# Bulk loads on one queue, q's place, products per unit and the gate's place in a convolution and attention kernel

## Chip, cores and metric

The kernel runs on one NeuronCore of a Trainium2 chip. The metric is the device time of one execution in microseconds (us). TensorE (PE) multiplies matrices into PSUM; VectorE (DVE) and ScalarE (ACT) copy and compute; GpSimd (POOL) prepares masks and, like SyncE (SP) and ACT, can issue DMAs. The 16 DMA engines move the data of all queues: POOL's issues go to queue q0, SP's to q1, ACT's to q10.

## The reference

All inputs are bf16, with S = 2048 positions and D = 640 channels. Here x is `A_q`, F a long convolution and att an attention over 8 keys.

```python
g = sigmoid((x * gate_w).sum(-1))
kv = (4-tap causal convolution of A_k with A_shift_k) * A_v
y = F(kv, A_ssm_k) + kv * A_ssm_D     # causal, as long as S, by FFT of length 2 S
a = x * y
b = att(x @ B_wqkv) @ B_wo            # 32 heads of 20; keys at i, i-2, ..., i-14
out = g * a + (1 - g) * b
```

## The kernel before

The program is written out by a planner. Each part of the work is a generator that yields requests (`Req`: engine, cost in ns, the events that it depends on, and for a DMA `move`, the time of its transfer). `Plan.run` (L195) takes the request with the smallest key, its earliest start plus 120 ns times a priority from `PRI` (L143), and only then the instruction is written into the program. So the planner's costs and due times set the order on every engine and every queue; on the chip each engine runs its list in order and waits for what the data need. The model of DMA has a `pipe` per queue (L158: SP, POOL and ACT apart) that transfers fill one after the other, and a `lane` of at most 8 transfers in flight.

The work in order of time:

- `loads` (L352) brings x and the weights in on SP. `heads` (L414) writes constants and masks on POOL. `xpose` transposes x on PE, and `vproj` (L512) and `qkproj` (L559) multiply it by the weights. The results of `qkproj` go through two staging tiles (`stg`).
- `fragger` (L598) moves rows of `stg` by 72 DMAs on SP, most of 20 rows and about 85 KB, to `qb` and `kb`: each head gets a place on 32 partitions. Four heads make a set, and there are 8 sets in three buffers.
- `score_gen` (L620) multiplies a set block by block, ACT takes exponentials (L627, 80 of them), and `pv_gen` (L648, L657, L660) multiplies by v and divides.
- `bulk` (L363) issues on POOL the loads of k, v and ssm_k (tile `h_lin`), 24 DMAs of 320 KB with contiguous pieces of 320, 160 and 128 bytes. `conv` (L465, L472) and `conv_v` (L476) compute kv on DVE.
- `gate` computes sigmoid. Its row goes by four small DMAs on SP (L535) from a part of tile `KX` to `g_nat`.
- `load_G` (POOL) puts the constant matrix G of the second stage into tile `SX`, columns 10240 to 18432. The transform of ssm_k of the first half (P = 0) lies in columns 0 to 10240. `load_T` (POOL) loads `wo` and the constant T.
- `h_stream` and `u_stream` (P = 0 and 1) transform ssm_k and kv: first stage `s1_unit` (L681), second stage `s2_unit` (L697), 11 units of 3 or 2 columns of 160 outputs, each copied out of PSUM by ACT or DVE (L274, L276). `swaps` (L768, L770) writes by DMA a copy `Hw` of the ssm_k side with its halves exchanged.
- `mults` (L781) multiplies on DVE the transforms: 16 products of 2560 elements a partition, each half P only after all of its transforms and its swaps.
- `inverse1` (L793) and `final` (L871) are the two stages back. `op_tr` (L811) and `outproj` (L827, L831) do the attention's output product, with 1 - g applied in ACT's copy.
- `load_q` (L843) loads x once more as `qg`, in 4 DMAs of 640 KB on POOL, into columns 0 to 10240 of `SX`. These hold data that `inverse1(0)` reads, so it waits for the last of that. `qscale` (L850) multiplies `qg` by g in 16 DVE instructions. For each of six groups of row tiles `final` copies out of PSUM on ACT (L878, two copies of up to 960 elements), multiplies by `qg` (L883), adds the attention's part (L885) and issues four DMAs on SP to the output (L888).

Of the kernel before, what the change touches and what calls it, by code (L numbers as in the profile page):

```python
# [47 lines left out]
WARM = 8  # L48

# [80 lines left out]
class Req:  # L130


    def __init__(self, engs, cost=0.0, deps=(), take=0, give=(), n=0, move=0.0, pri=None, mode=None, mm=0, lean=0.0):
        self.engs, self.cost, self.deps, self.take, self.give, self.n, self.move = engs, cost, deps, take, give, n, move
        self.pri, self.mode, self.mm, self.lean = pri, mode, mm, lean
# [14 lines left out]
class Plan:  # L150


    def __init__(self, nslots):
        self.at = dict(P=0.0, A=0.0, D=0.0, G=0.0, S=0.0, Q=0.0)
        self.mode = None
        self.count = 0
        self.page = 0.0
        self.pipe = {"S": 800.0, "G": 0.0, "Q": 0.0}  # L158
        self.lane = {"S": [], "G": [], "Q": []}
        self.slots = [Bank() for _ in range(nslots)]  # L160
        self.streams = []
        self.log = []
# [9 lines left out]
    def start(self, r, e):  # L172
# [10 lines left out]
        if r.move and len(self.lane[e]) >= 8:  # L183
            t = max(t, self.lane[e][-8])
        return t
# [9 lines left out]
    def run(self):  # L195
        while self.streams:
# [50 lines left out]
def kernel(  # L247
# [96 lines left out]
    def load(name, dst, src, us, deps=(), q="S"):  # L344
        g = yield Req(q, 700.0 if q != "G" else 300.0 + 0.7 * us, deps, move=us)
# [6 lines left out]
    def loads():  # L352
        yield from load_x(0)
        yield from load("Wv0", Wv[:, 0:3], W3[:, 0:3, 2, :], 1800.0)
        yield from load_x(1)
        yield from load("W0", Wqk[:, :, 0, :], W3[:, :, 0, :], 3000.0)
        yield from load_x(2)
        yield from load_x(3)
        yield from load("W1", Wqk[:, :, 1, :], W3[:, :, 1, :], 3000.0)
        for a in range(4, 8):  # L360
            yield from load_x(a)

    def bulk():  # L363
        for c in (1, 0):
            for q in range(4):
                yield from load(f"k{q}{c}", kin[32 * q:32 * q + 32, 3 + 32 * c:35 + 32 * c, :],
                                raw(k2, 32 * c * D + QC * q, [[64 * D, 32], [D, 32], [1, QC]]), 2200.0, [ev("x3")], "G")
# [9 lines left out]
        for c in range(2):  # L377
            for q in range(4):
                yield from load(f"v{q}{c}", vin[32 * q:32 * q + 32, c], raw(v2, QC * q + 80 * c, [[64 * D, 32], [D, 64], [1, 80]]), 2300.0, (), "G")
        yield Req("G", 1.0, [ev("xtr")])  # L380
        h_lin = p0.tile([128, 80, 2, 64], BF, name="h_lin", tag="HL")
        st["h_lin"] = h_lin
        for c in range(2):
            for q in range(4):
                yield from load(f"h{q}{c}", h_lin[32 * q:32 * q + 32, :, c, :],
                                raw(A_ssm_k, (160 * q + 80 * c) * S, [[64, 32], [S, 80], [1, 64]]), 2300.0, (), "G")

    def load_G():
        yield Req("G", 1.0, [ev("conv"), ev("grow"), ev("vproj")])
# [24 lines left out]
    def heads():  # L414
# [27 lines left out]
        plan.at["G"] = 19000.0  # L442
# [135 lines left out]
    def fragger():  # L578
# [4 lines left out]
        for ft in range(NDT):  # L583
            for w in range(2):
# [5 lines left out]
                for h in range(f0 // DH, (f0 + 127) // DH + 1):  # L590
# [6 lines left out]
                    g = yield Req("S", 720.0, deps, move=rows * 300.0 / eng)  # L597
# [109 lines left out]
    def transform(key, P):  # L707
# [109 lines left out]
    def outproj():  # L817
# [4 lines left out]
        for t in range(16):  # L822
# [14 lines left out]
    def load_q():  # L837
        yield Req("G", 1.0, [ev("i10")])
        qg = st["SX"][:, 0:16 * D].rearrange("p (t n) -> p t n", t=16)
        st["qg"] = qg  # L840
        for g in range(4):
            r = yield Req("G", 1200.0, move=2000.0)
            nc.gpsimd.dma_start(qg[32 * g:32 * g + 32], raw(x2, (32 * (g // 2) + g % 2) * D, [[64 * D, 32], [2 * D, 16], [1, D]]))  # L843
        mark("qg", r)

    def qscale():
        for t in range(16):
# [81 lines left out]
```

## Time and profile before

| | |
|---|---|
| median of 3 runs | 282.65 us (281.76 to 283.15) |
| the profiled execution | 282.82 us, its span 281.0 us |
| mean granted clock of PE | 0.84 |
| busy, share of the span | PE 77%, DVE 68%, ACT 58%, POOL 22% |
| DMA, share of 16 engines | q0 (POOL) 29.0%, 14.84 MB; q1 (SP) 26.3%, 18.04 MB |
| chain that ended last | PE 43%, DVE 26%, DMA 23%, SP's queue 3% |

The span is the profiled execution from its first to its last instruction. The chain is followed back from the last instruction to what released it at each step. A stretch of the span is shown with the busy time of each engine, the granted clock of PE (1.0 is full speed) and the share of time in which the DMA engines worked. A row of the timeline gives start, duration, engine, line, operation, output and input, and in brackets the idle time before it and what ended it.

### The profile page before, as it was taken

To read this page: it belongs to the slowest core of one execution; us is meant where nothing else is said; L and a number is where in the kernel's file an instruction comes from. 1 tells how busy PE (TensorE), PEld (TensorE's weight loads), DVE (VectorE), ACT (ScalarE), POOL (GpSimd) and SP (SyncE) were. 2 spreads that over 40 slices of the span, in tenths; PEclk is the share of its full clock that TensorE was granted. 3 is DMA by queue.
4 is the path that set the end of the run, shared out by engine and by line. 5 is a ranking of instruction groups with operands and counts; after the bars stand their busy time and mean duration, and the time that the engine had idled before them with its cause. 6 is when DMAs were issued, how large, how long until landed. Compare 5 with 4: busy or idle time off the path is not lost.

```text
span 281.0 us, 8233 instructions
## 1 busy us (share of the span) xinstructions
PE 216.7 (77%) x3654; PEld 166.9 (59%) x3654; DVE 189.8 (68%) x213; ACT 161.8 (58%) x197; POOL 60.5 (22%) x79
## 2 busy tenths in 40 slices
PE   6999999216900898999985999888999999991320
PEld 2999975103700466775663778777887789971210
DVE  2142079940502899999885878999998995411992
ACT  1333543033801387886884878999965588771460
POOL 5799999323301000000400000000000000300000
PEclk9999999755975599999955557999999999996555
DMA  6953999999995114233598100019579000495085
GB/s 221 333 208 81 168 169 166 157 166 200 153 101 84 25 42 89 52 72 76 159 266 243 51 3 2 3 39 220 122 155 220 5 0 2 87 197 94 11 213 156
DMA packets 13034, 33.81 MB, mean 120 GB/s; under 512 B 2764, under 2 KB 6872, under 8 KB 12360
## 3 DMA queue, kind: packets, MB, share of 16 engines
q0 software_dynamic: 4368, 14.84, 29.0%
q1 hardware_dynamic: 8072, 18.04, 26.3%
q8 instruction: 28, 0.46, 0.7%
q10 hardware_dynamic: 560, 0.42, 0.5%
q14 instruction: 6, 0.05, 0.1%
HBM read 20.01 MB, written 2.62 MB: 81 GB/s over the span
## 4 chain that ended last, share of the span: by engine, by line
PE 43%; DVE 26%; DMA 23%; SPq 3%; issue 2%; POOL 1%; ACT 1%; DVEq 0%
PE psv L512 9%; DMA kb<-stg 8%; PE op L827 7%; PE pj L559 6%; DMA g_nat<-KX 5%; DMA SX<-in_A_q_dram 5%; PE s L697 5%; DMA qb<-stg 5%; DVE UC L276 4%; PE sc L620 4%; PE i L793 4%; DVE Hs L276 3%; DVE stg L276 3%; DVE KX L465 3%; PE O L648 3%; DVE SX L885 2%
## 5 line engine op out<-in xcount | busy, mean ns | idle before, releaser
L627 ACT ACTIVATE ETall<-sc 121x912 bf16<-121x912 f32 (+1 forms) x80 | 64.3, 855 | 22.1 <-PE sc L620 21.2
L559 PE MATMUL pj<-xT,Wqk 128*128 128x342 bf16 (+1 forms) x300 | 51.6, 326 | 15.5 <-DVE oS L660 15.1
L559 PEld LDWEIGHTS <-Wqk 128*128 128x128 bf16 x300 | 28.8, 101 | 32.6 <-issue 16.4
L620 PE MATMUL sc<-qb,kb 31*128 31x114 bf16 x576 | 25.4, 242 | 18.0 <-DMA kb<-stg 16.8
L465 DVE TENSOR_TENSOR KX<-KX 128x1760 bf16<-128x1760 bf16 (+1 forms) x24 | 24.8, 1042 | 11.6 <-DMA KX<-in_A_k_dram 11.2
L620 PEld LDWEIGHTS <-kb 31*128 31x128 bf16 x576 | 14.6, 104 | 29.4 <-issue 20.0
L274 ACT CAST stg<-pj 128x684 bf16<-128x684 f32 (+1 forms) x13 | 9.5, 744 | 36.9 <-DMA kb<-stg 27.6
L472 DVE TENSOR_TENSOR KX<-KX 128x1760 bf16<-128x1760 bf16 (+1 forms) x18 | 18.8, 1044 | 15.9 <-DMA g_nat<-KX 15.4
L512 PE MATMUL psv<-KX,xT 128*121 128x320 bf16 x180 | 25.7, 299 | 1.4 <-DVE xT L276 1.4
L274 ACT CAST UC<-s 128x1024 bf16<-128x1024 f32 (+1 forms) x24 | 22.6, 1000 | 4.0 <-PE s L697 3.0
L512 PEld LDWEIGHTS <-xT 128*121 128x121 bf16 x180 | 23.6, 134 | 2.0 <-issue 1.2
L274 ACT CAST VW<-psv 121x640 bf16<-121x640 f32 x18 | 12.5, 695 | 21.0 <-PE psv L512 21.0
L827 PE MATMUL op<-wo,oT 128*128 128x512 bf16 (+1 forms) x160 | 23.5, 304 | 0.0
L697 PEld LDWEIGHTS <-SX 64*128 64x128 bf16 x512 | 20.2, 99 | 5.1 <-issue 3.3
L843 POOL DMA_DIRECT2D SX<-in_A_q_dram x4 | 2.6, 668 | 94.1 <-ACT UC L274 94.1
L276 DVE CAST stg<-pj 128x726 bf16<-128x726 f32 (+1 forms) x17 | 15.2, 894 | 11.1 <-DMA g_nat<-KX 10.3
L276 DVE CAST UC<-s 128x960 bf16<-128x960 f32 (+2 forms) x18 | 19.9, 1139 | 1.1 <-PE s L697 1.0
L276 DVE CAST SX<-s 128x1024 bf16<-128x1024 f32 (+1 forms) x16 | 18.8, 1195 | 2.5 <-PE s L697 1.9
L827 PEld LDWEIGHTS <-oT 128*128 128x128 bf16 x160 | 16.5, 147 | 5.7
L793 PE MATMUL i<-F,Hw 128*128 128x128 bf16 x160 | 18.3, 219 | 0.0
L831 ACT ACTIVATE bl<-op,omg 128x640 bf16<-128x640 f32 x16 | 12.7, 795 | 9.2 <-PE op L827 9.2
L793 PEld LDWEIGHTS <-Hw 128*128 128x128 bf16 x160 | 17.9, 113 | 0.0
(74 smaller groups left out, 370.4 us busy)
## 6 DMA issues: line engine op xcount, KB each, us to landing
xn<-in_A_q_dram SPq DMA_DIRECT2D x8, 320.0 KB
KX<-in_A_k_dram POOLq DMA_DIRECT2D x8, 320.0 KB, 9.7
vin<-in_A_v_dram POOLq DMA_DIRECT2D x8, 320.0 KB, 13.6
h_lin<-in_A_ssm_k_dram POOLq DMA_DIRECT2D x8, 320.0 KB, 17.2
Hw<-SX SPq DMA_DIRECT2D x4, 640.0 KB
Hw<-Hs SPq DMA_DIRECT2D x4, 640.0 KB
SX<-in_A_q_dram POOLq DMA_DIRECT2D x4, 640.0 KB, 10.2
out_dram<-SX SPq DMA_DIRECT2D x20, 120.0 KB
```

The costliest lines, as they stand in the source:

```text
L274: nc.scalar.copy(dst, src)
L276: nc.vector.tensor_copy(dst, src)
L465: eng.tensor_tensor(d, kin[:, n + 3 - j:n + 3 - j + m, :], w.to_broadcast([128, m, QC]), ALU.mult)
L472: eng.tensor_tensor(ta if j else dst, ta, tb, ALU.add)
L512: nc.tensor.matmul(ps[0:BK, n0 // 320, 0:320], lhsT=xT[:, dt, s0:s0 + BK], rhs=Wv[:, dt, n0:n1], start=(dt == 0), stop=(dt == NDT - 1))
L559: nc.tensor.matmul(ps[:, i, 0:n], lhsT=Wqk[:, dt, w, 128 * ft:128 * ft + 128], rhs=xT[:, dt, s0:s0 + n], start=(dt == 0), stop=(dt == NDT ...
L620: nc.tensor.matmul(sc[:, hh, BQ * bb:BQ * bb + BQ], lhsT=kb[r:r + DH + NF, BK * b:BK * b + 128], rhs=qb[r:r + DH + NF, BQ * b:BQ * b + BQ] ...
L627: nc.scalar.activation(ETall[0:BK, e, :, 0:BQ * nb], sc[0:BK, :, 0:BQ * nb], ACT.Exp, scale=SCALE)
L697: nc.tensor.matmul(ps[:, c, 160 * jj:160 * jj + 160], lhsT=st["G"][rows, j0 + jj, rr, :], rhs=Am[rows, rr].rearrange("p o (q j) l -> p j ( ...
L793: nc.tensor.matmul(d, lhsT=st[(key, P)][:, c, o + il // 4, :, il % 4], rhs=M[:, k, :], start=(k == 0), stop=(k == 1), skip_group_check=True)
L827: nc.tensor.matmul(op[:, n0:n1], lhsT=oT[:, ft].rearrange("p h m a -> p a (h m)")[:, t, :], rhs=wo[:, ft, n0:n1], start=(ft == 0), stop=(f ...
L831: nc.scalar.activation(bl[:, t, :], op[:, 0:D], ACT.Copy, scale=omg[:, t:t + 1])
```

## The change

k, v, ssm_k, G, wo, T and q are issued on SP instead of POOL. The planner now has a single `pipe` for all queues. A bulk load (one with `bg`) is placed no sooner than when the modelled backlog of the pipe is below BG = 1236 ns, and behind a request of priority 0 that could start at the same time. This is an order in SP's list; the program holds no wait for it. SP and ACT share one list of 8 transfers in flight. The new requests for G, wo, T, ssm_k and q on SP ("Req("S", 1.0, [...])") keep an issue behind its conditions in the plan.

q's tile `qg` moves to columns 8192 to 18432 of `SX`. Row tiles 4 to 15 lie in G's columns and are loaded when all four transforms' second stages are done, tiles 0 to 3 when `inverse1(0)` is done, each in four DMAs on SP. `final` and `outproj` take tiles 4 to 15 first.

`mults` becomes `products`: each unit of the second stage of kv is multiplied as soon as its copy and the swaps of its half P are done, 44 products of 960 or 640 elements in runs of 12 or 8.

`qscale` goes. `final` applies g as the per-partition scale of ACT's copies, which are now one for each row tile and half, 32 of 320 elements. All priorities and preferences of the planner (`PRI`, `LEAN_*`) have new values, and some modelled costs do.

```diff
+BG = 1236.0
...
-LEAN_QK = -370.0
-LEAN_V = 53.0
-LEAN_H = 195.0
-PRI = dict(loads=0, fragger=0, xpose=-8.5, score_gen=-1.4, pv_gen=1.9, conv=3.5, conv_v=5.1, bulk=0, conv_end=0, qkproj=2.0, vproj=-7.0, gate=5.7,
-           load_G=0, h_slot=0, u_slot=0, swaps=0, load_T=0, op_tr=6.4, outproj=4.9, load_q=0, qscale=0, final=11.8, h_stream=(2.5, 4.7),
-           u_stream=(5.8, -3.9), mults=(-7.4, 9.9), inverse1=(2.9, 1.2))
+LEAN_QK = 191.0
+LEAN_V = -60.0
+LEAN_H = 5.0
+PRI = dict(loads=0, fragger=0, xpose=0.2, score_gen=-1.6, pv_gen=-0.4, conv=4.7, conv_v=4.0, bulk=0, conv_end=0, qkproj=3.4, vproj=2.2, gate=4.4,
+           load_G=0, h_slot=0, u_slot=0, swaps=0, load_T=0, op_tr=-1.7, outproj=26.7, load_q=0, products=18.6, final=35.2, h_stream=(5.0, -0.2),
+           u_stream=(4.4, 22.6), inverse1=(22.6, -1.2))
...
-        self.pipe = {"S": 800.0, "G": 0.0, "Q": 0.0}
-        self.lane = {"S": [], "G": [], "Q": []}
+        self.pipe = 0.0
+        lane = []
+        self.lane = {"S": lane, "Q": lane, "G": []}
...
+        if r.bg is not None:
+            t = max(t, self.pipe - r.bg)
...
-                at = max(self.pipe[e], st + 1300.0)
-                self.pipe[e] = at + r.move
-                g.done = Ev(self.pipe[e] + 700.0, "X")
+                at = max(self.pipe, st + 1300.0)
+                self.pipe = at + r.move
+                g.done = Ev(self.pipe + 700.0, "X")
...
-    def load(name, dst, src, us, deps=(), q="S"):
-        g = yield Req(q, 700.0 if q != "G" else 300.0 + 0.7 * us, deps, move=us)
+    def load(name, dst, src, us, deps=(), bg=None, q="S"):
+        g = yield Req(q, 650.0, deps, move=us, bg=bg, pri=None if bg is None else 1)
         dict(S=nc.sync, Q=nc.scalar, G=nc.gpsimd)[q].dma_start(dst, src)
...
-    def bulk():
         for c in (1, 0):
             for q in range(4):
                 yield from load(f"k{q}{c}", kin[32 * q:32 * q + 32, 3 + 32 * c:35 + 32 * c, :],
-                                raw(k2, 32 * c * D + QC * q, [[64 * D, 32], [D, 32], [1, QC]]), 2200.0, [ev("x3")], "G")
+                                raw(k2, 32 * c * D + QC * q, [[64 * D, 32], [D, 32], [1, QC]]), 2000.0, (), BG)
+        for c in range(2):
+            for q in range(4):
+                yield from load(f"v{q}{c}", vin[32 * q:32 * q + 32, c], raw(v2, QC * q + 80 * c, [[64 * D, 32], [D, 64], [1, 80]]), 2300.0, (), BG)
+        yield Req("S", 1.0, [ev("xtr")])
+        h_lin = p0.tile([128, 80, 2, 64], BF, name="h_lin", tag="HL")
+        st["h_lin"] = h_lin
+        for c in range(2):
+            for q in range(4):
+                yield from load(f"h{q}{c}", h_lin[32 * q:32 * q + 32, :, c, :],
+                                raw(A_ssm_k, (160 * q + 80 * c) * S, [[64, 32], [S, 80], [1, 64]]), 2200.0, (), BG)
+
+    def bulk():
...
-        for c in range(2):
-            for q in range(4):
-                yield from load(f"v{q}{c}", vin[32 * q:32 * q + 32, c], raw(v2, QC * q + 80 * c, [[64 * D, 32], [D, 64], [1, 80]]), 2300.0, (), "G")
-        yield Req("G", 1.0, [ev("xtr")])
-        h_lin = p0.tile([128, 80, 2, 64], BF, name="h_lin", tag="HL")
-        st["h_lin"] = h_lin
-        for c in range(2):
-            for q in range(4):
-                yield from load(f"h{q}{c}", h_lin[32 * q:32 * q + 32, :, c, :],
-                                raw(A_ssm_k, (160 * q + 80 * c) * S, [[64, 32], [S, 80], [1, 64]]), 2300.0, (), "G")
...
-        yield Req("G", 1.0, [ev("conv"), ev("grow"), ev("vproj")])
+        yield Req("S", 1.0, [ev("conv"), ev("grow"), ev("vproj")])
...
-            yield from load(f"G{a}", G[:, 8 * a:8 * a + 8], cf["G"].ap().rearrange("p (a r b) -> p a r b", a=32, r=2)[:, 8 * a:8 * a + 8], 1600.0, (), "G")
+            yield from load(f"G{a}", G[:, 8 * a:8 * a + 8], cf["G"].ap().rearrange("p (a r b) -> p a r b", a=32, r=2)[:, 8 * a:8 * a + 8], 1700.0, (), BG)
...
-        yield Req("G", 1.0, [ev("p2")])
+        yield Req("S", 1.0, [ev("p2")])
...
-        yield from load("wo", wo[:], B_wo.rearrange("(t p) n -> p t n", p=128), 2400.0, (), "G")
-        yield Req("G", 1.0, [ev("hw0")])
+        yield from load("wo", wo[:], B_wo.rearrange("(t p) n -> p t n", p=128), 2700.0, (), BG)
+        yield Req("S", 1.0, [ev("hw0")])
...
-        yield from load("T", st["T"][:], cf["T"].ap().rearrange("p (a r b) -> p a r b", a=64, r=2), 2700.0, (), "G")
+        yield from load("T", st["T"][:], cf["T"].ap().rearrange("p (a r b) -> p a r b", a=64, r=2), 2700.0, (), BG)
...
-                    g = yield Req("S", 720.0, deps, move=rows * 300.0 / eng)
+                    g = yield Req("S", 720.0, deps, move=rows * 315.0 / eng)
...
+            if key == "u":
+                todo.append((P, j0, n, edone))
+                at(f"todo{len(todo)}", 0.0)
...
+    todo = []
+
+    def products():
+        for k in range(2 * len(JS)):
+            yield Req("D", 1.0, [ev(f"todo{k + 1}")])
+            P, j0, n, edone = todo[k]
+            for key in "hw":
+                r = yield Req("D", 150.0 + 0.53 * 320 * n, [edone, ev(f"hw{P}")])
+                X, U = [st[(x, P)][:].rearrange("p c o (q j) l -> p c (o q) (j l)", j=32)[:, :, :, 4 * j0:4 * j0 + 4 * n] for x in (key, "u")]
+                nc.vector.tensor_tensor(X, U, X, ALU.mult)
+            if k % len(JS) == len(JS) - 1:
+                mark(f"mult{P}", r)
...
-    MS = [(0, 0, 5), (0, 5, 10), (1, 0, 5), (1, 5, 10)]
-
-    def mults(P):
-        for c, l0, l1 in MS:
-            for key in "hw":
-                r = yield Req("D", 60.0 + 0.56 * 512 * (l1 - l0), outs("u", P) + outs("h", P) + [ev(f"hw{P}{c}")])
-                X, U = st[(key, P)], st[("u", P)]
-                nc.vector.tensor_tensor(X[:, c, l0:l1], U[:, c, l0:l1], X[:, c, l0:l1], ALU.mult)
-        mark(f"mult{P}", r)
...
-        for t in range(16):
+        for t in (*range(4, 16), *range(4)):
...
     def load_q():
-        yield Req("G", 1.0, [ev("i10")])
-        qg = st["SX"][:, 0:16 * D].rearrange("p (t n) -> p t n", t=16)
+        yield Req("S", 1.0, [ev(f"{k}s2{P}") for k in "hu" for P in range(2)])
+        qg = st["SX"][:, 8192:8192 + 16 * D].rearrange("p (t n) -> p t n", t=16)
         st["qg"] = qg
-        for g in range(4):
-            r = yield Req("G", 1200.0, move=2000.0)
-            nc.gpsimd.dma_start(qg[32 * g:32 * g + 32], raw(x2, (32 * (g // 2) + g % 2) * D, [[64 * D, 32], [2 * D, 16], [1, D]]))
-        mark("qg", r)
-
-    def qscale():
-        for t in range(16):
-            r = yield Req("D", 310.0, [ev("qg"), ev("gate")])
-            qg = st["qg"]
-            nc.vector.tensor_scalar(qg[:, t, :], qg[:, t, :], g_nat[:, t:t + 1], None, ALU.mult)
-            mark(f"qs{t}", r)
+        for n, (a, b) in enumerate(((4, 16), (0, 4))):
+            if n:
+                yield Req("S", 1.0, [ev("i10")])
+            for g in range(4):
+                r = yield Req("S", 650.0, move=550.0 + 120.0 * (b - a))
+                nc.sync.dma_start(qg[32 * g:32 * g + 32, a:b], raw(x2, (32 * (g // 2) + g % 2 + 2 * a) * D, [[64 * D, 32], [2 * D, b - a], [1, D]]))
+            mark(f"qg{a}", r)
...
-        for n, t0 in enumerate(range(0, 16, 3)):
-            m = min(3, 16 - t0)
+        for n, (t0, m) in enumerate(((4, 3), (7, 3), (10, 3), (13, 3), (0, 3), (3, 1))):
...
             yb = yb2[:, n % 2]
             es = []
             for k in range(2):
-                r = yield Req("A", 175.0 + 0.834 * 320 * m, [g.done, ybfree[n % 2]], give=[g.banks[k]])
-                nc.scalar.copy(yb[:, 0:m, 320 * k:320 * k + 320].rearrange("p n (q c) -> p q n c", q=2),
-                               pss[k][:, :, 0:160 * m].rearrange("p q (n c) -> p q n c", n=m))
+                for tt in range(m):
+                    r = yield Req("A", 175.0 + 0.834 * 320, [g.done, ybfree[n % 2], ev("gate")], give=[g.banks[k]] if tt == m - 1 else [])
+                    nc.scalar.activation(yb[:, tt, 320 * k:320 * k + 320].rearrange("p (q c) -> p q c", q=2),
+                                         pss[k][:, :, 160 * tt:160 * tt + 160], ACT.Copy, scale=g_nat[:, t0 + tt:t0 + tt + 1])
                 es.append(r.done)
-            reg = qg[:, t0:t0 + m, :]
-            yield Req("D", 60.0 + 0.58 * 640 * m, es + [ev(f"qs{t0 + m - 1}")])
+            yield Req("D", 150.0 + 0.53 * 640 * m, es + [ev("qg0" if t0 < 4 else "qg4")])
+            reg = st["qg"][:, t0:t0 + m, :]
             nc.vector.tensor_tensor(reg, yb[:, 0:m, :], reg, ALU.mult)
-            r = yield Req("D", 60.0 + 0.58 * 640 * m, [ev(f"bl{t0 + m - 1}")])
-            nc.vector.tensor_tensor(reg, reg, bl[:, t0:t0 + m, :], ALU.add)
+            r = yield Req("D", 150.0 + 0.53 * 640 * m, [ev(f"bl{t}") for t in range(t0, t0 + m)])
+            nc.vector.tensor_tensor(reg, reg, st["bl"][:, t0:t0 + m, :], ALU.add)
```

More of the change, by code (lines that the diff above doesn't have):

```diff
@@ L130, with __init__ @@
 class Req:
[L133 removed]
+    def __init__(self, engs, cost=0.0, deps=(), take=0, give=(), n=0, move=0.0, pri=None, mode=None, bg=None, mm=0, lean=0.0):
         self.engs, self.cost, self.deps, self.take, self.give, self.n, self.move = engs, cost, deps, take, give, n, move
[L135 removed]
+        self.pri, self.mode, self.bg, self.mm, self.lean = pri, mode, bg, mm, lean
 LAT = {("P", "A"): 230.0, ("P", "D"): 230.0, ("A", "P"): 120.0, ("D", "P"): 120.0, ("A", "D"): 100.0, ("D", "A"): 100.0}
 SWITCH = 110.0
[L140 to L145 removed]
+LEAN_QK = 191.0
[4 more added lines that the diff above has]
+           u_stream=(4.4, 22.6), inverse1=(22.6, -1.2))
 PAGE = 256
@@ L353, in loads @@
         yield from load_x(0)
-        yield from load("Wv0", Wv[:, 0:3], W3[:, 0:3, 2, :], 1800.0)
+        yield from load("Wv0", Wv[:, 0:3], W3[:, 0:3, 2, :], 1700.0)
         yield from load_x(1)
-        yield from load("W0", Wqk[:, :, 0, :], W3[:, :, 0, :], 3000.0)
+        yield from load("W0", Wqk[:, :, 0, :], W3[:, :, 0, :], 2800.0)
         yield from load_x(2)
         yield from load_x(3)
-        yield from load("W1", Wqk[:, :, 1, :], W3[:, :, 1, :], 3000.0)
+        yield from load("W1", Wqk[:, :, 1, :], W3[:, :, 1, :], 2800.0)
         for a in range(4, 8):
             yield from load_x(a)
-    def bulk():
         for c in (1, 0):
@@ L441, in heads @@
         plan.at["A"] = 3500.0
-        plan.at["G"] = 19000.0
+        plan.at["G"] = 17000.0
         plan.at["P"] = 3500.0
@@ L863, in final @@
                 pss.append(ps)
[L864 removed]
+            T, UC = st["T"], st["UC"]
             for tt in range(m):
@@ L892 @@
     for gen in (loads, fragger, xpose, score_gen, pv_gen, conv, bulk, conv_v, conv_end, qkproj, vproj, gate, load_G, h_slot,
-                u_slot, swaps, load_T, op_tr, outproj, load_q, qscale, final):
+                u_slot, swaps, load_T, op_tr, outproj, load_q, products, final):
         plan.add(gen(), PRI[gen.__name__])
-    for gen in (h_stream, u_stream, mults, inverse1):
+    for gen in (h_stream, u_stream, inverse1):
         for P in range(2):
```

1 line of the change is left out of this document (removed).

## Prediction

> **What bounds the kernel now.** I read the 40 slices first, then the stretches in time, the chain that ended last, and the rows of the tail. Four lines of the page (busy tenths in 40 slices of 7.0 us):
>
> ```profile
> PE   6999999216900898999985999888999999991320
> ...
> DVE  2142079940502899999885878999998995411992
> ...
> PEclk9999999755975599999955557999999999996555
> DMA  6953999999995114233598100019579000495085
> ```
>
> Counted from the left with 0, TensorE (PE) has holes in slices 7 to 9 and 11 to 12 and VectorE (DVE) in 8 to 12, PE's granted clock drops with them, and the DMA engines are full from slice 4 to 12. The stretches give sizes (us, then busy us of PE, PEld, DVE, ACT, POOL, the granted clock, DMA share, GB/s):
>
> ```profile
> 40.00:56.00 16.00, 10.78 (x85) 6.40 (x83) 15.59 (x15) 3.03 (x4) 10.86 (x11) 0.91 1.02 159
> 56.00:70.00 14.00, 5.39 (x44) 2.66 (x45) 3.60 (x5) 4.54 (x7) 4.41 (x4) 0.50 1.05 184
> 70.00:90.00 20.00, 7.52 (x142) 5.28 (x141) 4.51 (x6) 6.06 (x8) 2.37 (x2) 0.76 0.86 116
> 90.00:110.00 20.00, 16.59 (x245) 10.21 (x247) 18.92 (x25) 12.76 (x16) 1.28 (x1) 0.82 0.21 45
> ...
> 226.00:241.00 15.00, 15.00 (x225) 13.91 (x224) 10.75 (x8) 12.52 (x14) 0.00 (x0) 1.00 0.00 1
> 241.00:258.00 17.00, 11.53 (x292) 10.38 (x289) 3.67 (x3) 9.48 (x11) 2.64 (x4) 0.89 0.80 156
> 258.00:281.00 23.00, 5.42 (x371) 3.83 (x371) 16.85 (x28) 8.04 (x10) 0.00 (x0) 0.50 0.44 116
> ```
>
> From 56 to 90 us PE is busy 12.9 of 34 us and DVE 8.1, with DMA at 0.86 to 1.05. From 90 on compute is dense (PE 16.6 of 20, later 15.0 of 15). After 241 it is thin again. The chain of waits names both holes (start, length, what):
>
> ```profile
> 45.55 12.76 DMA qb<-stg
> 58.32 11.01 DMA kb<-stg
> ...
> 74.63 15.13 DMA g_nat<-KX
> ...
> 241.68 0.54 POOL SX L843
> ...
> 243.67 14.91 DMA SX<-in_A_q_dram
> ```
>
> So there are two DMA-bound places: the fragments (qb, kb) and g_nat, 38.9 us of chain between 45.5 and 89.8, and the late load of q, 14.9 us. Between them the engines bound the kernel.
>
> **Why the first place is slow.** A fragment of 85 KB lands 2.35 us after its issue where the chain meets one in quiet (108.25), but takes 11 to 13 us at 45 to 69. In that stretch GpSimd's queue q0 carries v and ssm_k, 5.2 MB. The packet records of the trace show how the two queues share: the 64-byte pieces of g_nat (issued by 75.1, landed at 89.8) start about 0.6 us apart near 78 to 80 us, in step with q0's packets of 4096 bytes, which take about 0.6 us there and 0.17 us at 134 to 146. The Trainium skill ("DMA: Bandwidth & Descriptors", Queues, rings and completion order) says that each DMA engine takes turns between queues, one packet at a time; the trace agrees.
>
> **The loads on SyncE (SP).** The bulk loads k, v, ssm_k become 24 issues on SP; G, wo, T and q add 14. The planner now holds them back to 1.236 us of modelled backlog. Only the order is written out; no wait is added to the program for the pace.
> - DMA time on q0: the records' median packet is 385 ns for 12 pieces of k (32 ns each), 409 for 26 of v (15.7), 364 for 32 of ssm_k (11.4). With 64, 128 and 160 pieces per engine and load this is 2.05, 2.0 and 1.8 us a load, 47 us for 24. On SP's queue no piece under 320 bytes but g_nat's is shown. ACT's hardware queue has pieces of 256 bytes at 17 ns and 470 at 26; an estimate by these (20, 13 and 12 ns) is 1.3, 1.7 and 1.9 us, 39 us in all. I take 47: those rows are of the same loads.
> - Start: SP's last x issue ends at 9.8, and the records show the loads of x and the weights over by 19.6. GpSimd issued k only at 25.0. So k, v and ssm_k could run from about 20 to 67, where before they lasted to about 87.
> - Fragments: SP's first issue is at 41.5, set 0 needs 11 issues at 0.72 (7.9 us), 2.35 to land: 52. The score matmuls on it ended their first wait at 61.0 and the last at 65.7. So 9 to 14 us sooner.
> - To the end of the hole: by 91.4 SP had issued 28 fragments. By SP's time these need 28 x 0.72 = 20.2, g_nat 4 x 0.52 = 2.1, and some 12 bulk issues between them at 0.65 (x's late issues took 0.81, the early ones 0.41) 7.8: 41.5 + 30.1 + 2.35 = 74. By DMA time: a 4.2 KB row takes about 0.31 us in quiet (records at 98 to 128 us), 20 rows on 10 engines 0.62, 28 of them 17.4 us; with 25 us of the 47 left at 41.5 this ends at 84. Since ssm_k is first read at 152.8 it can yield, so the value lies between 74 and 84, against 91.4.
> - g_nat's step shrinks from 15.1 towards 2.4 us; behind it on DVE are the convolution's products and the staging copies. Their work is not removed: next late are PE and DVE themselves.
> I take **-15 us** for the first place: the middle of 7 (91.4 less 84) and 22 (14 of set 0 and 8 of the 12.7 that g_nat's step loses). Ends: 0 and -26, the PE idle between 50.8 and 90 (39.2 less 12.9).
> - SP's other waits: G's load now waits on SP for the end of the convolution and the gate, 135.4 before. Fragments of the last heads stand behind it in program order (they ran to 146.1). The planner places it by due time, so I cost it at nothing; if it stands too soon each us is paid by the scores. wo and T landed 15.9 and 10.8 us after their issue at 138 and 147 and are first read at 210 and 250: covered.
>
> **q's place.** G is last read by the second stage's matmuls, which end at 212.0. q's tiles 4 to 15 go there at once, tiles 0 to 3 once inverse1(0) has ended. On SP the four issues follow the last Hw issue (ends 211.3). The q load of before took 241.7 to 258.6, 16.9 us for 2.62 MB; three quarters is 12.7, so it lands near 225, 27 us early. The last quarter, 4.2 us after 241.3, is needed near 265. Both hidden; if not, the tail is as before.
> The 16 scalings go (16 x 381 ns, 4.8 us, all on the path, 258.7 to 263.5). What is late next is ACT:
>
> ```profile
> 252.04 1.82 ACT L878 CAST yb<-i 128x960 bf16<-128x960 f32 x2
> 259.62 1.82 ACT L878 CAST yb<-i 128x960 bf16<-128x960 f32 x2 [5.76 <-PE i L871]
> ...
> 271.48 0.75 ACT L878 CAST yb<-i 128x320 bf16<-128x320 f32 x2 [0.44 <-DVE SX L883]
> ```
>
> The 12 copies (9.9 us) become 32 of 320 elements with g as scale. A plain one is 0.375 (last row). The scaled 640 of L831 takes 0.795 against 0.695 for a plain 640 of L274, so +0.10: 0.475; scaling 0.795 down by L878's slope gives 0.53. I take 0.50: 16 us. From the unchanged start 252.0 ACT ends at 268.0; DVE's last pair 0.97, then 5.2 from the last DVE end to the span's end (275.8 to 281.0): 274.2. DVE (12.3 us) and PE (6.9) fit beside it. **-6.8 us**; by 0.475 -7.6, by 0.53 -5.8.
>
> **Products per unit.** 16 of 2560 elements (1.48 us, 23.7 in all) become 44 of 960 or 640, runs of 12. At the old slope (1.48/2560 = 0.58 ns) 960 take 0.56 and up to 0.65 with a start cost: 24.6 to 28.6 us. If short runs ran as the PSUM copies of 960 do (1.15), about 50. I take 27: the L465 product over broadcast rows also keeps 0.59 ns an element. The Trainium skill ("VectorE: DVE Perf Modes", What auto-detection actually checks) asks for 16-bit tensors of step 1 and not for long runs, which gives 27; no run here shows runs of 12. The extra 3 us lie beside PE, which is full from 190 to 250 with transforms, outproj and inverse. They start sooner, but PE has no hole there to fill, so I cost it at **0** (-4 to +5). outproj's order only changes which row is first: 0.
>
> **Sum.** The profiled execution took 282.82 (span 281.0, 1.8 around it); the median is 282.65. 282.8 - 15 - 6.8 - 0 = 261.0; less 0.2 to the median, **260.8**.
>
> **Rivals.**
> - A, only the tail gains: the real loads do not follow the planner's pace, and SP stalls in its own issues. For: the third and fourth Hw issue took 2.39 and 2.37 us where the first took 0.54. At 1.8 us more for 16 bulk issues SP loses 29 us, the gain of the first place is gone: 276, between 270 and 283. The Trainium skill ("DMA: Bandwidth & Descriptors", Issuing engines are not separate DMA queues) says that the issuing engine saves only issue time; by that rule the DMA work stays and so would the hole. Against: v and ssm_k can go before and after the fragments.
> - B, slower: SP's hardware queue makes descriptors slowly, and fragments stand behind the loads in one queue. The fastest row shown is 1536 pieces in 7.8 us at 7 to 15 us, 5.1 ns each. k, v, ssm_k have 8 x (1024 + 2048 + 2560) = 45,056 pieces: 230 us at that, a run of some 400. But those engines were 78% busy with data, so the row is no limit. It decides from about 1.45 ns a piece (65 us in all, ending near 85, with the 6.8 won in the tail against it); q0 did 1.04. At 2 ns, 90 us: 25 us later, about 300.
> - C, products at 50 us: DVE has 6 us free between 174 and 241; 26 more cost about 15: 276.
>
> **Chances.** Forecast 0.58 (range of its own 249 to 270), A 0.20, B 0.16, C 0.06. A change under 0.5% can't be told from none. Faster: 0.58 + 0.18 of A + 0.04 of C = 0.80; same 0.04; slower 0.16. The range reaches from both large gains (-26, -7.6, -4: 245) to A and C, 280; outside are B and a little of A.
>
> **What would show it.** Right: first score matmul near 52, no DMA step over 6 us in the chain at 45 to 90, g_nat landing in 3 us, all exponentials ended some 15 us before 169.8; in the tail no wait for q, ACT full after inverse1(1) with copies near 0.5 us, last output about 22 us after the first copy. Wrong: ssm_k loads over 4 us each on SP's queue (B), bulk issues over 2 us on SP (A), products near 1.1 us (C), or the hole gone but the score stage ending no sooner, since PE or DVE bounds it.

## The result, and the profile after

The changed kernel takes **257.3 us** (median of 4 runs, 255.1 to 258.2) against 282.8 before in the same comparison (281.8 to 283.2): a ratio of 0.909, 95% interval 0.903 to 0.916. The forecast was 260.8. The profiled execution took 256.9, its span 255.0. Of b1 and c3, two runs of four each were over 1.5% slower than their fastest, the profiled ones among them: the ratios leave the slow runs out, the medians do not, and from these two profiles I use the order, the transfers and the early stages.

The same four lines of the page as were shown of before (busy tenths in 40 slices, now of 6.4 us):

```profile
PE   7899999998939999575699998999999989996320
...
DVE  1244699998579998865588979999974999453691
...
PEclk9999999999988999799555559999999999999555
DMA  7999576994552699899592000000799999600474
```

The two holes of PE and DVE in the first third are gone but for one slice of PE at 70 to 76 us (there the score matmuls wait 3.86 us for DVE's copy into `stg`), and the granted clock no longer falls there. The loads that stood in one block are spread to slice 18, 121 us; behind them come G and wo. The stretches (us, busy us of PE, PEld, DVE, ACT, POOL, granted clock, DMA share, GB/s):

```profile
40.00:56.00 16.00, 15.91 (x230) 12.54 (x229) 15.16 (x19) 10.62 (x14) 0.00 (x0) 1.00 1.03 142
56.00:70.00 14.00, 12.45 (x132) 7.10 (x130) 9.96 (x11) 7.14 (x9) 0.00 (x0) 1.00 0.59 107
70.00:90.00 20.00, 15.16 (x307) 10.69 (x307) 17.56 (x26) 12.67 (x18) 0.00 (x0) 0.91 0.53 101
90.00:110.00 20.00, 16.78 (x230) 10.62 (x230) 17.20 (x23) 10.24 (x14) 0.00 (x0) 0.91 0.89 142
110.00:130.00 20.00, 13.67 (x292) 10.00 (x291) 12.68 (x16) 13.57 (x19) 0.93 (x1) 0.81 1.04 146
...
232.00:255.00 23.00, 5.69 (x414) 3.98 (x397) 12.47 (x12) 13.64 (x32) 0.00 (x0) 0.56 0.46 117
```

From 56 to 90 us PE is busy 27.6 of 34 us where it was 12.9. A smaller DMA-bound place has appeared at 110 to 130. The chain that ended last names it, and one more (start, length, what):

```profile
110.95 10.66 DMA h_lin<-in_A_ssm_k_dram
...
182.62 12.22 DMA Hw<-SX
...
232.44 1.90 issue
...
235.83 2.51 issue
```

The trace follows this chain back only to 91.8 us; from there on no transfer of a fragment, of g_nat or of q is among its long pieces. SP's issues of fragments do stand in it from 100.3 to 108.7, about 0.7 us each, ahead of the late ssm_k load. Earlier, the waits of the score matmuls show the same: the longest for a fragment between 42 and 92 us is 0.82 (a later one, at 105.6, is 2.66). SP's queue in the order of time shows how the loads now stand among the fragments:

```profile
29.29 5.46 SPq L602 DMA_DIRECT2D qb<-stg  x7
34.79 1.04 SPq L350 DMA_DIRECT2D KX<-in_A_k_dram  x2
37.69 5.23 SPq L602 DMA_DIRECT2D kb<-stg  x7
42.96 0.44 SPq L350 DMA_DIRECT2D KX<-in_A_k_dram  x1
43.45 10.69 SPq L350 DMA_DIRECT2D vin<-in_A_v_dram  x5
...
88.26 2.09 SPq L350 DMA_DIRECT2D h_lin<-in_A_ssm_k_dram  x2
90.46 4.74 SPq L602 DMA_DIRECT2D qb<-stg  x5
95.26 2.16 SPq L350 DMA_DIRECT2D h_lin<-in_A_ssm_k_dram  x2
```

Where the 26.0 us between the two spans (281.0 and 255.0) came from: the last attention step began at 171.0 and now at 150.3, **20.7** sooner. From there to the first copy of the last stage it was 81.0 and is 81.6, **0.6** longer. From that copy to the end it was 28.9 and is 23.0, **5.9** shorter. The attention step before, then the same step and the first copy in the changed kernel:

```profile
171.02 0.66 DVE L660 TENSOR_TENSOR oS<-O,rd 114x480 bf16<-114x480 f32 x1
```

```profile
150.34 0.66 DVE L664 TENSOR_TENSOR oS<-O,rd 114x480 bf16<-114x480 f32 x1
...
231.95 2.61 ACT L884 ACTIVATE yb<-i,g_nat 128x320 bf16<-128x320 f32 x6
```

One trace places such a step only within a few microseconds: a5, a6, a7, c1 and c2 below run the same lists as the changed kernel up to that attention step, and there it begins between 147.8 and 152.0.

### The profile page after: what moved, and what is told of

Same layout as the page of the kernel before. It is cut to its first block, busy times and chain, and to the rows that moved or that the text cites. A ratio compares the mean times of both kernels' runs of the same rounds, so it can differ in the third digit from the quotient of the medians.

```text
span 255.0 us, 8256 instructions
## 1 busy us (share of the span) xinstructions
PE 215.1 (84%) x3654; PEld 167.9 (66%) x3654; DVE 190.2 (75%) x230; ACT 162.8 (64%) x212; POOL 29.9 (12%) x45
## 4 chain that ended last, share of the span: by engine, by line
PE 23%; DVE 17%; DMA 9%; SPq 5%; ACT 4%; issue 3%; POOLq 0%; ACTq 0%; DVEq 0%
PE i L803 7%; DVE SX L280 6%; DMA Hw<-SX 5%; DMA h_lin<-in_A_ssm_k_dram 4%; PE sc L624 3%; SPq L602 3%; PE O L652 3%; DVE SX L739 2%; DVE Hw L739 2%; PE s L701 2%; PE op L837 2%; ACT yb L884 2%; PE s L685 2%; PE tr L821 2%; PE i L876 1%
## 5 line engine op out<-in xcount | busy, mean ns | idle before, releaser
L563 PE MATMUL pj<-xT,Wqk 128*128 128x342 bf16 (+1 forms) x300 | 50.4, 319 | 0.6 <-ACT ETall L631 0.6
L278 ACT CAST UC<-s 128x960 bf16<-128x960 f32 (+2 forms) x32 | 29.0, 993 | 0.8 <-PE s L701 0.4
L516 PE MATMUL psv<-KX,xT 128*121 128x320 bf16 x180 | 27.3, 300 | 1.0 <-DVE xT L280 1.0
L280 DVE CAST stg<-pj 128x684 bf16<-128x684 f32 (+1 forms) x20 | 17.7, 884 | 11.2 <-PE pj L563 8.8
L280 DVE CAST SX<-s 128x1024 bf16<-128x1024 f32 (+2 forms) x19 | 21.0, 1163 | 5.2 <-PE s L685 5.1
L278 ACT CAST VW<-psv 121x640 bf16<-121x640 f32 x14 | 9.7, 694 | 22.3 <-PE psv L516 22.3
L278 ACT CAST UC<-i 128x1024 bf16<-128x1024 f32 x17 | 16.2, 1021 | 4.9 <-PE i L803 3.4
L652 PEld LDWEIGHTS <-ETall 121*128 121x128 bf16 x576 | 16.4, 100 | 2.4 <-issue 1.3
L652 PE MATMUL O<-VW,ETall 121*128 121x21 bf16 x576 | 17.5, 176 | 0.3 <-DVE oS L664 0.2
L280 DVE CAST Hs<-s 128x1024 bf16<-128x1024 f32 (+1 forms) x14 | 16.5, 1202 | 1.0 <-PE s L701 0.8
```

Of the source, the lines that this page charges most:

```text
L278: nc.scalar.copy(dst, src)
L280: nc.vector.tensor_copy(dst, src)
L516: nc.tensor.matmul(ps[0:BK, n0 // 320, 0:320], lhsT=xT[:, dt, s0:s0 + BK], rhs=Wv[:, dt, n0:n1], start=(dt == 0), stop=(dt == NDT - 1))
L563: nc.tensor.matmul(ps[:, i, 0:n], lhsT=Wqk[:, dt, w, 128 * ft:128 * ft + 128], rhs=xT[:, dt, s0:s0 + n], start=(dt == 0), stop=(dt == NDT ...
L652: nc.tensor.matmul(O[:, (b - b0) // 6, c0:c0 + 21], lhsT=ETall[0:BK, e, hh, BQ * bb:BQ * bb + 128], rhs=VW[0:BK, b, 4 * t + h4, :], start= ...
```

## The experiments

All kernels do the whole computation. Ratios are to the kernel before, each with its 95% interval; the times are medians of four runs, of a4 ten.

**a1, a2, a3: which part of the plan makes the gain.** a1 gives three of the planner's priorities their old values, so that the projections of v and of q and k stand in their old order:

```diff
-PRI = dict(... xpose=0.2, ... qkproj=3.4, vproj=2.2, ...)
+PRI = dict(... xpose=-8.5, ... qkproj=2.0, vproj=-7.0, ...)
```

a2 keeps the new priorities and takes the functions `loads`, `bulk`, `load_G` and `load_T` and the planner's model of DMA from before (24 bulk loads, G, wo and T on POOL, no pace; q stays on SP). a3 does both.

> The changed kernel with the three priorities of xpose, vproj and qkproj set back to those before, so that vproj runs before qkproj and the first fragment leaves near 41 us instead of 29. Theory 1 (the bulk loads' place on SP and their pace made the fragments fast, the start hardly matters since the engines bound the rest): the last exponential within 5 us of the changed kernel's 148, time 257 to 262 us. Rival 2 (the gain of the first place is the earlier start of the fragments): attention ends some 10 us later, time 266 to 270 us.

> The changed kernel with k, v, ssm_k, G, wo and T issued on POOL again, with the planner's separate pipes and no pace; q, products, gate and all priorities stay as changed. Theory 1: fragments take turns with POOL's packets again, landing 8 us or more after issue, attention ends 12 to 20 us later, time 270 to 278 us. Rival 2: the fragments still leave early, time 257 to 263 us.

> Both edits: loads on POOL and vproj first. What is left of the change is the tail, the products and the other priorities. Theory 1 and rival 2 both say that the first place is back as before: 274 to 279 us (282.8 less 4 to 8). If it is 265 or less, something else than loads and start made the gain.

Measured: a1 261.2 (0.930, 0.927 to 0.933), a2 274.3 (0.976, 0.970 to 0.981), a3 276.6 (0.985, 0.980 to 0.990). By the times, the loads dealt out on SP are worth 17 us with the new order of the projections (a2 against the changed kernel) and 15 with the old (a3 against a1); the order is worth 4 us with the loads on SP and 2 with them on POOL. All the other edits together give 4 to 6 (a3 against before). In a1 the first fragment leaves at 42.8 and the first score starts at 52.3, in the changed kernel at 29.3 and 43.8; the last attention step begins only 2.1 us later (152.4 against 150.3), less than the spread named above, and in a2 12.6 us later (162.9). Not all of the difference lies before that step: from there to the first copy of the last stage a1 takes 84.5 us and a2 87.1, the changed kernel 81.6. What lengthens this stretch was not tested. Nor was a kernel run with the loads on POOL and dealt out by a pace of their own. In a2, with POOL's loads beside them, g_nat's four small DMAs hold SP for 14.5 us, in the changed kernel for 5.2 (SP's queue of a2: start, busy us, four issues):

```profile
79.25 14.45 SPq L536 DMA_DIRECT2D g_nat<-KX  x4
```

**b1: the loads alone.** The kernel before, with only the 24 loads, G, wo and T on SP, the pace and the planner's one pipe.

> The kernel before with only the loads of k, v, ssm_k, G, wo and T on SP with the pace and the planner's one pipe; old priorities, q late on POOL, old products, gate on DVE. Theory 1: 15 to 20 us faster, 263 to 268 us. Rival 2: under 5 us, 278 to 283 us.

Measured: 274.2 (0.963, 0.958 to 0.967), between the ranges of its theory (263 to 268) and its rival (278 to 283): both missed. The last attention step begins at 155.2 instead of 171.0, **15.8 us sooner**, but by the ratio the run ends only some 10.5 us sooner. In the profiled execution, which ends 4.3 us sooner, the stretch from that step to the first copy of the last stage takes 89.7 us instead of 81.0 and the tail 31.8 instead of 28.9. Why the stretch is longer was not tested; the tail's long wait is still there (chain):

```profile
239.62 14.60 DMA SX<-in_A_q_dram
```

**a4: the pace.** The changed kernel with the holding back taken out, so that SP's list has all 24 loads ahead of the fragments:

```diff
-                                raw(k2, 32 * c * D + QC * q, [[64 * D, 32], [D, 32], [1, QC]]), 2000.0, (), BG)
+                                raw(k2, 32 * c * D + QC * q, [[64 * D, 32], [D, 32], [1, QC]]), 2000.0)
```

The same goes for v, ssm_k, G, wo and T.

> The changed kernel with the pace taken out (no backlog limit for the bulk loads, same priority as the fragments), loads still on SP. If the pace is what keeps the fragments fast (theory 1): v and ssm_k are issued ahead of the first fragments, these land 10 us or more after issue, time 264 to 275 us. Rival 3 (it is enough that one queue carries all, since the loads are done sooner): 255 to 260 us.

Measured: **282.5 (1.000, 0.997 to 1.004)**: the whole gain is gone, more than the theory's 264 to 275 allowed. SP's queue (start, busy us):

```profile
10.78 18.51 SPq L350 DMA_DIRECT2D KX<-in_A_k_dram  x8
29.34 19.41 SPq L350 DMA_DIRECT2D vin<-in_A_v_dram  x8
48.87 16.35 SPq L350 DMA_DIRECT2D h_lin<-in_A_ssm_k_dram  x8
65.33 7.29 SPq L602 DMA_DIRECT2D qb<-stg  x7
```

Each issue takes 2.0 to 2.4 us where one in quiet takes 0.4 to 0.7, and the first fragment leaves at 65.3 instead of 29.3. The loads move the same bytes through the same queue in both; only their place in the lists differs. That is rival A's mechanism, and rival B's condition as well, since the fragments now stand behind the loads: the 24 issues take SP 54.3 us, while the loads take 68.4 us of DMA time and land by 70.1, so a4 does not part the two. The Trainium skill ("DMA: Bandwidth & Descriptors", Issuing engines are not separate DMA queues) says that another issuing engine saves only issue time. For the move by itself these runs show no gain, but a loss of 8 us: a4 against a2, 274.3, where the loads are on POOL and all else is alike but the planner's model of DMA and some modelled costs. The gain comes from what the move allows, an order.

**a5, a6, c2: the tail.** a5 puts the gate back on DVE: 16 scalings of q and 12 plain copies, q early. a6 keeps the gate in ACT's copies and puts q into its old columns, all eight DMAs on SP behind inverse1(0). c2 does both.

a5 and c2 (`qscale` and the two copies of each group as before, one DVE scaling a row tile):

```diff
-                    nc.scalar.activation(yb[:, tt, 320 * k:320 * k + 320].rearrange("p (q c) -> p q c", q=2),
-                                         pss[k][:, :, 160 * tt:160 * tt + 160], ACT.Copy, scale=g_nat[:, t0 + tt:t0 + tt + 1])
+                nc.scalar.copy(yb[:, 0:m, 320 * k:320 * k + 320].rearrange("p n (q c) -> p q n c", q=2),
+                               pss[k][:, :, 0:160 * m].rearrange("p q (n c) -> p q n c", n=m))
...
+            nc.vector.tensor_scalar(qg[:, t, :], qg[:, t, :], g_nat[:, t:t + 1], None, ALU.mult)
```

a6 and c2:

```diff
-        yield Req("S", 1.0, [ev(f"{k}s2{P}") for k in "hu" for P in range(2)])
-        qg = st["SX"][:, 8192:8192 + 16 * D].rearrange("p (t n) -> p t n", t=16)
+        yield Req("S", 1.0, [ev("i10")])
+        qg = st["SX"][:, 0:16 * D].rearrange("p (t n) -> p t n", t=16)
```

> The changed kernel with g multiplied into q on VectorE again (16 scalings of 640, as before) and 12 plain copies on ScalarE instead of 32 scaled ones; q stays early in the freed matrix. Theory: the early q is the gain of the tail, the scalings hide behind the inverse stages, the copies fall from 13.9 to 10 us: 254 to 258 us, at most 2 us from the changed kernel. Rival: moving the gate is itself half of the gain (4.8 us of scalings left the path): 260 to 263 us.

> The changed kernel with q's tile in its old columns, loaded in the same 8 DMAs on SP but only after inverse1(0). By the trace of the changed kernel inverse1(0) ends near 219 and the first product with q starts at 234.6; a load of 17 us ends at 236.5: 2 to 4 us slower, 259 to 262 us. Rival (forecast: the late load is worth the tail's whole gain): 263 to 266 us.

> The changed kernel with both tail edits taken back together: q in its old columns, loaded by SP after inverse1(0), and the gate as 16 scalings on DVE with 12 plain copies on ACT. All work is done. Each edit taken back alone cost nothing (255.0 and 256.9 against 257.3). Theory (the tail needs one of the two, since late q and its scalings stand in one chain): q issued at 218 to 222, landed some 17 us later near 236 to 239, the 16 scalings of 0.38 run after that, 4.8 to 6 us, so the first q product comes near 238 to 241 instead of 234: 260 to 265. Rival (the new order of the stages alone hides q, with or without scalings): 255 to 258.

Measured: a5 255.0 (0.906, 0.901 to 0.912), a6 256.9 (0.913, 0.907 to 0.919), c2 258.5 (0.913, 0.907 to 0.918). Neither edit brings anything that these runs can tell, and the two together at most a microsecond or two (the intervals of c2, a5 and the changed kernel overlap). a6 lies below both of its ranges, whose lowest value was 259. c2 missed its theory's 260 to 265 and lies half a microsecond above its rival's 255 to 258, though the chain of events was the expected one (SP's issues, and DVE, which waits for q, scales it and then multiplies):

```profile
220.86 3.99 SPq L854 DMA_DIRECT2D SX<-in_A_q_dram  x8
...
234.47 4.83 DVE L861 TENSOR_SCALAR SX<-SX,g_nat 128x640 bf16<-128x640 bf16 x16 [2.87 <-DMA SX<-in_A_q_dram]
239.21 1.15 DVE L893 TENSOR_TENSOR SX<-yb,SX 128x1920 bf16<-128x1920 bf16 x1
```

The first product starts at 239.2 instead of 234.6, and yet DVE ends at 251.7 instead of 249.8, in a run whose attention had already ended 1.7 us later. From 239.2 on DVE multiplies without a gap (12.5 us), while in the changed kernel it waits for ACT 6.3 us in between. The groups of the changed kernel from 225 us on show for what (busy us, mean ns, idle before and who ended it):

```profile
L884 ACT ACTIVATE yb<-i,g_nat 128x320 bf16<-128x320 f32 x32 | 13.7, 561 | 1.8 <-PE i L876 1.6
L876 PE MATMUL i<-UC,T 32*32 32x160 bf16 x512 | 6.8, 281 | 6.8 <-issue 5.2 <-ACT yb L884 1.6
...
L889 DVE TENSOR_TENSOR SX<-yb,SX 128x1920 bf16<-128x1920 bf16 (+1 forms) x6 | 6.3, 1046 | 6.3 <-ACT yb L884 6.3
```

PE's pauses of the kind "issue" (5.2 us) and ACT's copies, busy 13.7 of the 15.3 us from the first to the last, pace the tail, so an early q only waits. The pauses are not the same in every run: in a4, whose last stage is the changed kernel's, they come to 0.4 us, ACT's copies follow each other without a gap, and the tail takes 21.1 us (the same two groups of a4):

```profile
L884 ACT ACTIVATE yb<-i,g_nat 128x320 bf16<-128x320 f32 x32 | 13.5, 641 | 0.1
L876 PE MATMUL i<-UC,T 32*32 32x160 bf16 x512 | 6.6, 239 | 5.2 <-ACT yb L884 4.8 <-issue 0.4
```

So with the gate in ACT's copies ACT is the engine that bounds the tail, and with the gate on DVE (c2) it is DVE. What PE's pauses are, no run shows.

**a7 and c1: the products.** a7 restores the 16 products of 2560 elements with a place of their own in the plan, each after its whole half. c1 has the same 16 products, but in the place of the 44, behind the last copy of the second stage:

```diff
-        for k in range(2 * len(JS)):
-            yield Req("D", 1.0, [ev(f"todo{k + 1}")])
...
+        for P in range(2):
+            yield Req("D", 1.0, [ev(f"todo{len(JS) * (P + 1)}")])
...
+            for c, l0, l1 in ((0, 0, 5), (0, 5, 10), (1, 0, 5), (1, 5, 10)):
...
+                    nc.vector.tensor_tensor(X[:, c, l0:l1], U[:, c, l0:l1], X[:, c, l0:l1], ALU.mult)
```

Their modelled cost in c1 is the same in sum.

> The changed kernel with the 16 products of 2560 elements after all transforms of a half instead of 44 per unit. In the changed kernel's trace the first product waits for the swapped copy Hw (landed 194.8) and not for its unit, so the unit size can give little: forecast 0, 256 to 259 us. Rival (products per unit let the inverse start sooner): 261 us or more.

> The changed kernel with its 44 products replaced by 16 of 2560 elements at the same place in DVE's list: one row behind the last copy of the second stage, with the same planned total. All work is done. Theory (the 4 us that the run with the old products lost came from their place on DVE, ahead of a copy of the second stage, not from their size): 256 to 258 us, the row of products about 22.5 us long (16 at the old pace of 1.40) instead of 24.5 (43 at 0.57), so the first copy of the last stage is at most 2 us sooner. Rival (starting unit by unit is what gains: the product of the first unit lets inverse1 begin sooner, or spreads the DVE load): 260 to 262, with PE waiting for DVE between 190 and 200 as with the old products.

Measured: a7 261.4 (0.926, 0.919 to 0.932), c1 **254.7 (0.904, 0.898 to 0.910)**. a7's time is its rival's (261 or more), not the forecast 256 to 259; c1 came out below both of its ranges, whose lowest value was 256. a7 loses by its place: DVE's products stand ahead of a copy that frees PSUM, and PE is busy 5.27 of the 10 us from 190 to 200, against 9.98 in the changed kernel (stretch of a7):

```profile
190.00:200.00 10.00, 5.27 (x102) 4.50 (x97) 9.59 (x9) 6.29 (x7) 0.00 (x0) 0.84 1.00 213
```

The size of the products is no gain, as c1 shows, which has the same products without that loss. In the changed kernel the 44 products run in one row, held up at its start by the swapped copy; in c1 they are not. DVE of the changed kernel, then of c1:

```profile
187.75 3.29 DVE L280 CAST UC<-s 128x960 bf16<-128x960 f32 x3 [1.31 <-PE s L701]
195.03 0.66 DVE L739 TENSOR_TENSOR SX<-UC,SX 128x960 bf16<-128x960 bf16 x1 [4.00 <-DMA Hw<-SX]
195.60 0.65 DVE L739 TENSOR_TENSOR Hw<-UC,Hw 128x960 bf16<-128x960 bf16 x1
```

```profile
185.57 2.21 DVE L280 CAST UC<-s 128x960 bf16<-128x960 f32 x2
187.70 1.48 DVE L740 TENSOR_TENSOR SX<-UC,SX 128x2560 bf16<-128x2560 bf16 x1
189.10 1.48 DVE L740 TENSOR_TENSOR Hw<-UC,Hw 128x2560 bf16<-128x2560 bf16 x1
```

A unit's columns lie in all parts of the matrix, so its product waits for all four swap DMAs of its half; a quarter by channels lies in one c and needs two of them. That is 4.0 us of waiting, and 22.5 us instead of 24.5 for the row. Counted from the last attention step, the last stage's first matmul starts after 78.8 us in c1 and after 80.6 in the changed kernel (79.9 to 80.6 in a5, a6, c2 and c3, which have the 44 products too). The times alone do not tell c1 from the changed kernel: the intervals overlap. Of the other 4.1 us by which c1's profiled span is shorter, 2.6 were there at the last attention step, before the edit acts, and 1.5 fall in the tail.

**c3 and c4: the late ssm_k.** c3 loads the two halves of ssm_k in the opposite order. c4 is a5 with the ssm_k loads held back less:

```diff
-        for c in range(2):
+        for c in (1, 0):
...
-                                raw(A_ssm_k, (160 * q + 80 * c) * S, [[64, 32], [S, 80], [1, 64]]), 2200.0, (), BG)
+                                raw(A_ssm_k, (160 * q + 80 * c) * S, [[64, 32], [S, 80], [1, 64]]), 2200.0, (), 4000.0)
```

The first pair is c3's, the second c4's.

> The changed kernel with the two halves of ssm_k loaded in the opposite order; nothing else stands differently in any engine's list. All work is done. In the changed kernel the first four loads (first half of channels) took 2.07 us of DMA time each, the last four 3.1 to 5.1. Theory (the price belongs to the half: where its pieces of 128 bytes are read or written): now the first four take 3.1 to 5.1 and the last four 2.1. Rival (it belongs to the time or to what runs beside it): the first four again near 2.1 and the last four 3 to 5. The time by both: 255 to 259.

> The version with the gate on DVE (255.0), with the held-back distance of the eight ssm_k loads raised from 1.236 to 4 us of backlog, so that SP issues them sooner among the fragments. All work is done. In the changed kernel TensorE waits 4.0 us at 118.5 to 122.9 for the last ssm_k load and GpSimd's add on it. Theory (this wait is on the path): it goes to under 1 us and the run ends 1 to 4 us sooner than 255.0: 251 to 254. Rival (sooner ssm_k loads delay fragments by as much, or the scores bound the stage anyway): 254 to 258, with the last attention no sooner than 149.4.

Measured: c3 257.3 (0.899, 0.893 to 0.906), c4 256.8 (0.910, 0.905 to 0.914). In c4 GpSimd's add runs at 119.8 instead of 120.9 and PE's wait of 4.0 us for it is gone, but the last attention step begins at 150.0, in a5 at 149.4, and the time is no better: the rival holds. PE waits elsewhere instead: at 106.5 it waits 4.26 us for ACT's copy into `stg` and at 108.3 another 1.28 for a fragment, where a5 waits 2.90 for a fragment at 104.4. Since the add came only about 1 us sooner, c4 tests the late ssm_k no further than that. c3's time is within its range; its transfers belong to the last section.

## Why the prediction was right, and where it was not

**The first place, -15 us.** It came out at -20.7. The loads by themselves are worth the forecast value there (b1: -15.8, though only some 10.5 by the end of the run). The other 4.9 us are a term that the prediction had not sized, and they fit the rest of the plan: in a3, with loads and projections as before, the last attention step begins at 166.1, 4.9 us sooner than before. The new priorities also start the projections of q and k at 16 us instead of 36 and the first fragment at 29.3; by a1 that is worth 2.1 us, which one trace cannot tell from nothing. With the old order of the projections the first score starts at 52.3 (a1), where the prediction had put it, 52.

The working behind the value was partly wrong. The DMA time of the 24 loads is 61 us by the records (k 17.0, v 19.3, ssm_k 24.7), not 47, and the loads were not over at 67 but at 120. That did little harm, since most of it lies beside compute, between fragments. The prediction took the order for granted ("v and ssm_k can go before and after the fragments"); a4 shows that the whole gain hung on this sentence. So that this value came out near is in part luck: the DMA time was put too low by 14 us, and the loads' place beside compute made up for it.

**Waits of G, wo and T on SP, 0.** Right: G is issued at 124.9, behind the last fragment of a head (SP's row of fragments before it ends at 124.6). What the step left out is ssm_k, which became late: 4.0 us of PE's time and a 10.7 us step in the chain, but c4, which brings it about 1 us forward, shows nothing won there.

**The tail, -6.8.** It measured -5.9, in part from another cause, so the near hit is in part luck. The step "q's early place and no scalings" fails: taken back alone and together (a5, a6, c2) it is worth nothing that these runs can tell. What brings the gain shows in c2, which has neither edit and a tail of 23.1 us from the first copy, as long as the changed kernel's 23.0. There q lands 13.6 us after its first issue on SP, and the first copy comes 13.3 us after that issue; before it was 16.9 on POOL, and 10.4. So q is 0.4 us late where it was 6.6, a gain of 6.2. That this much comes from SP's queue (3.3) and from the new order around inverse1 (2.9) is read from the two traces; no run parts them. "ACT is late next" held: from the first copy to the last ACT takes 15.3 us, where the prediction had 16. But the copies take 0.43 each, not 0.50 (13.7 us in all), and waits for PE, which pauses, make up most of the rest; in a4, almost without them, the tail is 21.1.

**Products, 0.** Held within its bounds (-4 to +5). They cost 0.57 each, so short runs keep the fast rate; the Trainium skill's list of conditions ("VectorE: DVE Perf Modes", What auto-detection actually checks) gave the same. "They start sooner" was wrong: they start later than they could, on the swaps. By c1's trace, counted from the last attention step, the split costs about 2 us.

**The rivals.** A is real when the loads are not held back, and a4's 282.5 lies in its range (270 to 283), with the tail's gain still in it: a4's last attention step begins at 173.4, 2.4 us later than before. Its sign, issues over 2 us, is there at 11 to 23 and 43 to 54 us in the changed kernel too; no fragment was ready then, but for the last half microsecond. B's price was nearer than I gave it: 61 us for 45,056 pieces is 1.35 ns a piece, and it was to decide from 1.45. It decides only if the loads stand as a block in front of the fragments. In a4 they do: there their 68.4 us are 1.52 ns a piece, and the gain is gone. C is refuted by 0.57 against 1.1.

## What to carry to other kernels

A load on the queue of small urgent transfers is neither good nor bad: with the same bytes on the same queue the run took 257 us with the loads dealt out among the fragments and 282 with them in front. So ask of each bulk transfer what stands behind it in the issuing engine's list, and when that is due. And before a gain is credited to an edit that looks as if it caused it, take that edit back alone and together with its neighbour: here the early q and the moved gate were worth nothing that could be measured, apart or together.

## What the runs showed of the hardware that was not expected

The price of a small piece depends on which half of the tensor is moved. All ssm_k loads are 320 KB in pieces of 128 bytes; c = 0 and c = 1 differ in the channels read and in the place in the tile's rows (the first or the second 128 of 256 bytes). From the packet records, us of DMA time a load, in the order of issue:

```
changed kernel:  c=0  2.07 2.07 2.07 2.09   c=1  3.29 3.14 5.07 4.89
c3 (reversed):   c=1  3.03 4.86 3.06 5.07   c=0  3.35 2.07 2.08 2.08
c4 (sooner):     c=0  2.07 2.09 2.11 2.07   c=1  3.13 4.76 3.08 5.08
```

The dear half stays dear when it goes first, so the time and what runs beside it are not the cause of the difference; a load right behind one of the dear half is dearer still, c3's first c = 0 load (3.35) too. Whether the reading or the writing side does it was not tried.

An issue on SP is not a fixed cost: 0.4 to 0.7 us in quiet, 2.0 to 2.4 with a backlog on the queue (a4). And in the last 20 us of the scores PE runs at a granted clock of 0.50 in the kernel before (150 to 170), in the changed one (130 to 150) and in a4 (150 to 170), though it is busy 9.1 to 10 of each 10 us; this phase lies in all three and moves with the stage, so its presence explains no difference between them.
